# Memory attention and SwiGLU on one core: four pairs of batches swept as a wave, in an order that a table sets

## The chip, the cores and the metric

One NeuronCore of a Trainium2 chip runs one program. Its five engines have queues of their own and meet at semaphores: TensorE (PE in the profile, PEld for its weight loads), VectorE (DVE), ScalarE (ACT), GpSimd (POOL), and SyncE (SP), which issues every DMA of this kernel. The metric is the device time of one execution in microseconds (us), lower is better.

## The reference

Eight batches of eight heads attend through 32 memory slots a head; the result goes, token by token, through a gated feed-forward layer. q and k are scaled up by 200, so that the scores are sharp.

```python
a = softmax(phi, axis=2)                       # over the 576 positions
k_m, v_m = a^T k, a^T v                        # 32 x 64 a head
attn = softmax(q k_m^T / 8)                    # 576 x 32
x = (attn v_m), heads side by side             # 4608 tokens x 512
xn = x / sqrt(mean(x^2) + 1e-6) * rms_g
out = (silu(xn w_gate) * (xn w_val)) w_out     # d_ff = 1536
```

All inputs are float32 but the three weight matrices, which arrive as float64 (the kernel reads them as pairs of 32-bit words).

## The kernel before, in words

Two batches make a pair, so there are four pairs. For each pair three things are done.

**Preparation.** For each batch b: `prep` (L485) takes the maximum of phi over the positions (`mc`, then `mt` and `mr` by transposes through PE), subtracts it, and `e_bd` holds the exponentials; `kv_steps` (L556) multiplies them with k and v into `kvp`, adds the sums (`es`), normalizes (`si`, `im`, `kb`, `vb`) and turns the result (`kvt`); `km` serves the scores, `vg` and `vm` (split into a high and a low part) the sweep, `gram` the norm.

**Attention.** q is turned (`qtp`, `qT`), scored against `km` (`S`), and its softmax (`mxs` or `mx`, `ex`, `sm`) is `a`. `x_steps` (L168) turns `a` (`tp`, `at`), gets the square sum of each token by `xp` and `ssq`, takes the inverse root in `fin` (L262) by a bit trick and four Newton steps (L278) on all nine columns at once, spreads it over `at` (`rp`), and splits the result into `ath` and `atl`.

**Sweep.** An item is one pair and one of twelve columns of 128 hidden units; there are 48. `vw_steps` (L824) multiplies the values into the weights (`vp`, evacuated as `xh` on ACT and `xl` on DVE), `gv_steps` (L872) makes gate and value (`pg`, `pv`), `sg` = silu on ACT, `hf` = the product on DVE, and its split `hh` (ACT) and `hl` (POOL). After each second item `out_steps` (L918) multiplies by the two rows of w_out: nine tiles `po` of six matmuls, added into `acc` on DVE (copied on ACT the first time). All of the sweep's products are made three times over, high by high, high by low and low by high, to keep float32 accuracy.

Each weight column is made from float64 once (`convert`, L340): two passes on ACT, three on DVE (`ex`, L350, L359, L366), one addition of integers (`w`, L379, on DVE but for two on POOL), a high part on ACT and a low part on POOL (`wh`, `wl`, `oh`, `ol`, L396 and L397). It is written to DRAM (`wd`, `od`) and read again by `reload` (L410) when its buffers have been given to others: there are two sets of each.

The work stands in two stages. In the first (L422 to L803) all eight batches are prepared and pairs 0 and 1 attend, with `kv`, `q` and PSUM pools of its own. What pairs 2 and 3 need later goes through DRAM (`vgd`, `gd`). Then the pools close, and the sweep begins. It runs over pairs 0 and 1 together (two items of pair 0, two of pair 1, with the same two columns, then the next columns), and after twelve columns over pairs 2 and 3 (`where`, L817). Pairs 2 and 3 attend between the items of the first half (`attend_steps`, L959; `x2`, L1035). The place of each step is a number in `PRM` (L26): the steps are sorted by it (L802, L1088), and the framework's scheduler makes each engine's queue out of that.

Of the kernel before, what the change touches and what calls it, by code (L numbers as in the profile page):

```python
# [19 lines left out]
XTTR = True  # L20

# [3 lines left out]
WB = 3  # L25
PRM = dict(  # L26
    K_AT=[12.08, 15.05, 41.68, 67.52, 100.72, 122.69, 147.6, 167.28],
    KP=0.82,
    POST=[-0.15, 3.05, 3.9, 7.72, 15.27, 21.96],
    P1=4.13,  # L30
    PREP=[-1.56, 0.79, 2.32, 3.9, 18.7],
    PD=[2.1, 11.67, 7.79, 18.42, 7.54, 2.17],
    EXP=[1.89, 13.89, 3.07, 6.96, 11.93, 1.72],
    ES=1.16,
    PH=[9.86, 15.89, 41.23, 73.43, 103.91, 132.92],
    S_AT=[32.67, 47.44, 51.02, 69.42, 103.56, 112.2, 119.41, 123.39],
    KD=[-29.43, -117.84, -35.71, -6.98, -5.97, -14.4, 0.19, -2.47, -27.9, -16.32, -19.75, -7.2, -11.66, -11.87, -26.49, -25.1, -22.49, -18.77, -23.35, -24.43, -11.42, -13.48, -5.56, -9.46, -16.01, -22.32, -10.3, -18.0, -66.41, -9.39, -2.35, -17.36],
    QD=[5.05, 6, 3, 5, 23.44, 20.6, 19, 15.8],
    PD0=0.96,
    QL=3.73,  # L40
    OL=3.83,
    QO=[-0.32, 1.73, -1.7, 0.7, 1.27, 3.23],
    SO=[3.76, 13.53, 20.6, 28.62],
    X_AT=[102.5, 152.9],
    XP=1.78,
    LAG=0.79,
    CV=114.79,
    CP=3.53,
    CV2=155.67,
    CP2=0.05,  # L50
    QE=[0, 0],
    CE=[2, 1],
    XE=[28, 29, 14, 13],
    ESN=[3, 3, 2, 3, 3, 3, 2, 3],
    SUM=[1, 0, 1, 0, 2, 1, 2, 1],
    CA=1,
    B=[2, 2, 2],
    RO=3.35,
    RS=4.63,
    RP=2.84,  # L60
    GV=[0.12, 0.256, 0.267, 0.683, 0.84, 0.979],
    VW=[-0.204, 0.03, 0.165],
    VW0=0.296,
    O=[0.115, 0.297, 0.451, 0.524, 0.954, 0.957, 1.344, 1.487, 1.518],
    PRE=[-0.525, 1.142, 1.893, 2.147, 2.545, 2.788],
    PI=0.0157,
    PSW=[1.728, 2.047, 2.009, 2.653, 2.96, 3.24],
    SU=[1.874, 3.014, 5.716, 6.6, 9.746, 12.208, 13.357, 15.533],
    AO=[0.162, 0.169, 0.192, 0.276, 0.385, 0.474, 0.562, 0.581, 0.59, 0.601, 0.728, 0.804, 1.158, 1.217],
    XB=[17.199, 22.916],  # L70
    XS=[0.1086, 0.0359],
    XM=[21.887, 24.858],
    XN=[0.012, 0.176, 0.184, 0.33, 0.33, 0.566, 0.596, 0.699, 0.766],
    LV=[22.571, 24.198],
    CB=1,
)


def weave(*lists):

    order = []
    for li, entry in enumerate(lists):
        steps, lo, hi = entry if isinstance(entry, tuple) else (entry, 0.0, 1.0)
        n = len(steps)
        for i, s in enumerate(steps):
            order.append((lo + (hi - lo) * (i + 0.5) / n, li, i, s))
    order.sort(key=lambda e: e[:3])  # L90
    for e in order:
        e[3]()
# [3 lines left out]
def kernel(  # L96
# [12 lines left out]

    nc = tc.nc
    P = 128
# [17 lines left out]
    vm = {}  # L141
    gram = {}
    gb = persist.tile([P, 2, 2, P], F32, name="gb")
    dram = ctx.enter_context(tc.tile_pool(name="dram", bufs=1, space=bass.MemoryType.DRAM))
    gram_dram = {i: dram.tile([P, 2, 2, 64], F32, name=f"gd{i}") for i in range(G, NP)}
    a_dram = {i: dram.tile([P, NT, 256], F32, name=f"ad{i}") for i in range(G, NP)}
    rinv = [persist.tile([P, NT], F32, name=f"rinv{i}") for i in range(NP)]
    at_hi, at_lo = {}, {}

    vg_dram = {b: dram.tile([P, HP, 64], F32, name=f"vgd{b}") for b in range(2 * G, B)}  # L150
    km_late = {b: persist.tile([P, HP, 64], F32, name=f"km{b}") for b in range(2 * G, B)}
    ssqs = {}
# [6 lines left out]
    def split_v(b, vg):
        pr, j = divmod(b, 2)  # L160
        for e in range(2):
            o = e ^ j
            src = vg.rearrange("p (c e) m -> p c e m", e=2)[:, :, o, :]
            hi, lo = vm[pr][:, 0, :, e, o, :], vm[pr][:, 1, :, e, o, :]
            nc.scalar.copy(hi, src)
            nc.gpsimd.tensor_tensor(out=lo, in0=src, in1=hi.bitcast(F32), op=ALU.subtract)

    def x_steps(pr, a, psum_t, psum_x, fetch=None):  # L168

        tps, xps, srcs, st = {}, {}, {}, {}  # L170
        i = pr % G

        def first():
            st["at"] = persist.tile([P, NT, 2, P], F32, tag="at", name=f"at{pr}")
            ssqs[pr] = persist.tile([P, NT], F32, tag=f"ssq{i}", name=f"ssq{pr}")
            for par in range(2):
                rows = slice(64 * par, 64 * par + 64)
                (nc.scalar.copy if pr < G else nc.sync.dma_start)(gb[rows, :, :, rows], gram[pr][rows])
# [941 lines left out]
```

## Time and profile before

| | us |
|---|---|
| median of 3 runs (lowest, highest) | 899.51 (896.29, 899.54) |
| the profiled execution, device time | 896.89 |
| its span, first to last instruction | 895.1 |
| mean granted PE clock | 0.978 |

Times in the profile are counted from the span's start. A timeline row gives the start and the length in us, engine, line and operation, "out<-in", the shape and how many; what ended an idle time stands in brackets. A row by groups ends in "busy us, mean ns of one | idle before". A row by windows gives each engine's busy us and its instructions, then the granted PE clock, the share of the DMA engines and GB/s. The profile counts a float32 matmul twice (it is done in two passes); the order counts it once.

### The profile page before, as it was taken

Reading aid. Unit: us, or ns where it says so; the run is one execution under the profiler, and the core shown is the slowest. Engines: PE = TensorE matmul, PEld = TensorE weight load, DVE = VectorE, ACT = ScalarE, POOL = GpSimd, SP = SyncE. Lnnn points to the kernel's source line nnn. Section 1 sums busy time; section 2 is a strip of 40 time slices with the busy share of each in tenths; the row PEclk is TensorE's granted clock in tenths of the full one; section 3 lists DMA queues with packets and bytes.
Section 4 is the critical chain, followed back from the end, with each engine's and each line's share of the span. In section 5 each row is a group of like instructions: output and inputs, shape, how many; then the busy total and the mean of one; then the engine's idle time right before and its main releaser. Section 6 shows DMA issues by size and latency. Waiting matters only on the chain.

```text
span 895.1 us, 15791 instructions
## 1 busy us (share of the span) xinstructions
PE 835.6 (93%) x6207; PEld 741.3 (83%) x6207; DVE 559.0 (62%) x956; ACT 422.0 (47%) x719; POOL 286.7 (32%) x242
## 2 busy tenths in 40 slices
PE   4989586999998999999999999899999999999997
PEld 4777476899987988897788997898889999999996
DVE  5577958985778868878845746622545555455543
ACT  2666435787765645656532532344333323333330
POOL 3463735533524414323422421511211112211120
PEclk9899788999999999999999999999999999999999
DMA  8987553652644422534222143502204012040046
GB/s 292 320 263 239 204 169 101 223 168 60 217 114 153 150 61 95 163 105 142 102 73 93 60 117 102 135 1 72 70 4 139 1 63 79 1 142 1 9 110 141
DMA packets 81506, 106.41 MB, mean 119 GB/s; under 512 B 34324, under 2 KB 52248, under 8 KB 81432
## 3 DMA queue, kind: packets, MB, share of 16 engines
q1 hardware_dynamic: 81432, 105.41, 38.0%
q8 instruction: 49, 0.80, 0.4%
q14 instruction: 25, 0.20, 0.1%
HBM read 73.93 MB, written 31.46 MB: 118 GB/s over the span
## 4 chain that ended last, share of the span: by engine, by line
PE 74%; DVE 10%; issue 5%; DMA 5%; ACT 4%; POOL 1%; SPq 1%; DVEq 0%; POOLq 0%; ACTq 0%
PE po L932 29%; PE pv L890 15%; PE pg L890 14%; PE vp L843 6%; PE kvp L567 3%; DMA phi<-in_phi_dram 2%; PE xp L240 2%; DVE w L379 2%; DVE xl L868 1%; DVE ex L350 1%; DMA raw<-in_moe_w_out_dram 1%; PE qtp L679 1%; PE S L700 1%; DVE acc L939 1%; DVE mc L493 1%
## 5 line engine op out<-in xcount | busy, mean ns | idle before, releaser
L913 POOL TENSOR_TENSOR hl<-hf,hh 128x512 fp32r<-128x512 f32 (+1 forms) x96 | 141.4, 1474 | 405.9 <-ACT hh L912 392.3
L939 DVE TENSOR_TENSOR acc<-po,acc 128x512 f32<-128x512 f32 x180 | 123.1, 687 | 128.2 <-PE po L932 127.6
L932 PE MATMUL po<-oh,hh 128*128 128x512 f32 x432 | 172.4, 400 | 3.0 <-DVE acc L939 2.0
L932 PE MATMUL po<-oh,hl 128*128 128x512 f32 x432 | 170.6, 395 | 0.0
L932 PE MATMUL po<-ol,hh 128*128 128x512 f32 x432 | 170.4, 394 | 0.0
L898 ACT ACTIVATE sg<-pg 128x256 f32<-128x256 f32 x192 | 78.1, 411 | 163.2 <-PE pg L890 151.6
L868 DVE TENSOR_TENSOR xl<-vp,xh 64x1024 fp32r<-64x1024 f32 x94 | 114.7, 1220 | 52.3 <-ACT xh L867 51.2
L899 DVE TENSOR_TENSOR hf<-pv,sg 128x256 f32<-128x256 f32 x192 | 85.2, 452 | 71.6 <-PE pv L890 49.0
L867 ACT CAST xh<-vp 64x1024 fp32r<-64x1024 f32 x94 | 94.8, 1008 | 49.7 <-PE vp L843 23.9
L912 ACT CAST hh<-hf 128x512 fp32r<-128x512 f32 (+1 forms) x96 | 64.7, 674 | 81.9 <-DVE hf L899 59.5
L932 PEld LDWEIGHTS po<-oh,hl 128*128 128x128 f32 x432 | 81.2, 188 | 19.3
L932 PEld LDWEIGHTS po<-oh,hh 128*128 128x128 f32 x432 | 81.1, 188 | 17.0 <-DVE acc L939 2.9
L890 PE MATMUL pg<-ath,xh 128*128 128x320 f32 (+1 forms) x384 | 87.3, 300 | 5.7 <-ACT sg L898 3.0
L932 PEld LDWEIGHTS po<-ol,hh 128*128 128x128 f32 x432 | 81.3, 188 | 11.0
L843 PE MATMUL vp<-wh,vm 128*128 128x256 f32 x384 | 85.4, 286 | 3.6 <-DVE xl L868 2.8
L890 PE MATMUL pv<-ath,xh 128*128 128x320 f32 (+1 forms) x384 | 85.0, 299 | 1.1 <-DVE hf L899 0.9
L890 PE MATMUL pg<-atl,xh 128*128 128x320 f32 (+1 forms) x384 | 84.9, 297 | 0.0
L890 PE MATMUL pg<-ath,xl 128*128 128x320 f32 (+1 forms) x384 | 84.7, 295 | 0.0
L890 PE MATMUL pv<-atl,xh 128*128 128x320 f32 (+1 forms) x384 | 84.5, 296 | 0.0
L890 PE MATMUL pv<-ath,xl 128*128 128x320 f32 (+1 forms) x384 | 83.2, 296 | 0.0
L890 PEld LDWEIGHTS pg<-ath,xh 128*128 128x128 f32 x384 | 63.5, 189 | 12.0 <-ACT sg L898 4.8
L843 PEld LDWEIGHTS vp<-wh,vm 128*128 128x128 f32 x384 | 65.4, 189 | 6.7 <-DVE xl L868 2.3
(129 smaller groups left out, 1338.3 us busy)
## 6 DMA issues: line engine op xcount, KB each, us to landing
kv<-in_k_dram SPq DMA_DIRECT2D x32, 288.0 KB, 5.2
kv<-in_v_dram SPq DMA_DIRECT2D x32, 288.0 KB, 5.8
out_dram<-acc SPq DMA_DIRECT2D x72, 128.0 KB, 2.4
raw<-in_moe_w_gate_dram SPq DMA_DIRECT2D x12, 512.0 KB, 5.0
raw<-in_moe_w_val_dram SPq DMA_DIRECT2D x12, 512.0 KB, 3.9
wd<-wh SPq DMA_DIRECT2D x12, 512.0 KB, 3.4
wd<-wl SPq DMA_DIRECT2D x12, 512.0 KB, 4.2
raw<-in_moe_w_out_dram SPq DMA_DIRECT2D x12, 512.0 KB, 4.2
```

The lines of the kernel that those rows point to most:

```text
L240: nc.tensor.matmul(xp[64 * j:64 * j + 64, P * cc:P * cc + P], st["at"][:, t, cc, 64 * j:64 * j + 64], gb[:, j, cc], start=True, stop=True,)
L567: nc.tensor.matmul(kvp[64 * par:64 * par + 64, cc, 0:128], e_bd[j][:, hp, c, :], st["kv", b, hp][:, :, 64 * c:64 * c + 64], start=(c == 0) ...
L843: nc.tensor.matmul(vp[:, e, :], lhs(l), r[:, 2 * cc + e, :], start=(n == 0), stop=(n == 2),)
L867: nc.scalar.copy(xh[rows], src)
L868: nc.vector.tensor_tensor(out=xl[rows], in0=src, in1=xh[rows].bitcast(F32), op=ALU.subtract)
L890: nc.tensor.matmul(pt[:, :N], l[:, cc, b, half * P:half * P + P], r[:, b, cc, t0:t0 + n, :].rearrange("p t x -> p (t x)"), start=(m == 0), ...
L898: nc.scalar.activation(sg[:, :N], pg[:, :N], AF.Silu)
L899: nc.vector.tensor_tensor(out=hf[:, :, b, :], in0=pv[:, :N].rearrange("p (t x) -> p t x", x=64), in1=sg[:, :N].rearrange("p (t x) -> p t x ...
L912: nc.scalar.copy(hh, hv)
L913: nc.gpsimd.tensor_tensor(out=hl, in0=hv, in1=hh.bitcast(F32), op=ALU.subtract)
L932: nc.tensor.matmul(po, l[:, tt, :], r, start=(m == 0), stop=(m == 5))
L939: nc.vector.tensor_tensor(out=accs[key], in0=po, in1=accs[key], op=ALU.add)
```

## The change

One pool arrangement serves from the first instruction on. Only pair 0's two batches are prepared and only pair 0 attends ahead of the sweep, in early pools; pairs 1, 2 and 3 are prepared, with the narrow buffers of the sweep, while earlier pairs are swept. Sweep entries (a pair and two columns) follow `ORDER`: four of pair 0, then one of pair 1, one of pair 0, and so on; the first one or two entries of a pair lie between the last ones of its forerunner. The columns are converted as pair 0 needs them, and each later use reads them from DRAM. Every step is now one part of a list (mostly one instruction each), and `ISSUE`, 3,127 numbers, gives the order in which they are issued; the scheduler is off. Smaller edits: the integer addition of `convert` is on POOL always; the inverse root is taken in two pieces (four tiles, five tiles) with three Newton steps each; the second pair's q comes by the four strided loads of the late pairs; softmax sums are always one reduction on DVE; the sums of `phi`'s exponentials always use three POOL additions; `gram` and `vg` stay on the chip.

```diff
-G = 2
+ORDER = [
+    (0, 0), (0, 1), (0, 2), (0, 3), (1, 0), (0, 4), (1, 1), (0, 5), (1, 2), (1, 3), (1, 4), (2, 0), (1, 5), (2, 1), (2, 2), (2, 3), (2, 4), (3, 0), (2, 5), (3, 1), (3, 2), (3, 3), (3, 4), (3, 5),
+]
+ISSUE = [
+    13, 33, 14, 15, 16, 34, 17, 18, 38, 1, 2, 3, 19, 4, 5, 20, 6, 8, 7, 9, 39, 40, 10, 48, 41, 22, 11, 49,
...
+def perform(tc, parts):
+    assert sorted(ISSUE) == list(range(len(parts)))
+    with tc.manual_schedule():
+        for n in ISSUE:
+            parts[n]()
...
     def where(i):
-        ps_, r = divmod(i, NU * G * 2)
-        u, r = divmod(r, G * 2)
-        pi, f = divmod(r, 2)
-        return ps_, u, ps_ * G + pi, 2 * u + f
+        p, u = ORDER[i // 2]
+        return p, u, 2 * u + i % 2
...
-            on_pool = n < 2 and kind < 2 and PRM["CE"][n] & (1 << kind)
-            (nc.gpsimd if on_pool else V).tensor_tensor(out=d["w"].bitcast(I32), in0=d["m"], in1=d["ex"], op=ALU.add)
+            nc.gpsimd.tensor_tensor(out=d["w"].bitcast(I32), in0=d["m"], in1=d["ex"], op=ALU.add)
...
-            for _ in range(4):
+            return [f0, f1, f2, f3, f4] + [newton(a) for a in range(3)]
...
+            if t == 3:
+                steps.append(fin(0, 4))
+        steps.append(fin(4, NT))
...
+    for n in range(NS):
+        new = first_use[where(n)[1]] == n // 2
+        for kind in range(3) if new else (0, 2):
+            if new:
+                add(lambda kind=kind, n=n: load_w(kind, n), convert(kind, n))
+            else:
+                add(lambda kind=kind, n=n: reload(kind, n))
```

The queues show it at three places. On PE, before the first gate product `pg0` (item 0), this stood before; `rp1` belongs to pair 1's inverse root, `kvt7` to the last batch, `vp0` and `vp1` to items 0 and 1:

```order
L209 MATMUL rp1_4_1762<-ident_58,rinv1_71 128x128 x4
L611 MATMUL kvt7_1747<-ident_58,kb7_1743 128x128 x2
L611 MATMUL kvt7_1747<-ident_58,vb7_1744 128x128 x2
L209 MATMUL rp1_8_1768<-ident_58,rinv1_71 128x128
L636 MATMUL kvt7_1747<-vt7_1758 64x64 x4
L843 MATMUL vp0_0_1804<-wh0_1361,vm0_456 128x256
...
L843 MATMUL vp1_1839<-wh1_1714,vm0_456 128x256
L890 MATMUL pg0_00_1847<-ath0_1391,xh0_1818 128x256
```

And this stands there now (`rp0` is pair 0's inverse root, `kvt2` and `kvp3` batches 2 and 3, which are pair 1):

```order
L784 MATMUL rp0_4_973<-ident_72,rinv0_105 128x128 x4
L784 MATMUL rp0_8_987<-ident_72,rinv0_105 128x128
L498 MATMUL kvt2_992<-ident_72,kb2_828 128x128 x2
L498 MATMUL kvt2_992<-ident_72,vb2_824 128x128 x2
L459 MATMUL kvp3_0_887<-ones_109,es3_819 64x1 x2
...
L445 MATMUL kvp3_1_1024<-kv3_3_942,e_bd1_123 64x128
...
L1071 MATMUL pg0_10_1053<-ath0_970,xh0_723 128x320 x2
```

Item 0's first gate product stood behind eight batches and two attending pairs, and stands behind four batches and one attending pair.

On POOL, around items 2 and 3 (`hl` is the low part of the product, `wl` and `ol` the low parts of a weight column, `ex` an attention tile), before:

```order
L397 TENSOR_TENSOR wl3_2312<-w0_3_2230,wh3_2311 128x4x128
L397 TENSOR_TENSOR wl3_2312<-w1_3_2274,wh3_2311 128x4x128
L913 TENSOR_TENSOR hl2_0_2164<-hf2_0_2105,hh2_0_2163 128x512
L913 TENSOR_TENSOR hl2_1_2316<-hf2_1_2240,hh2_1_2315 128x640
L913 TENSOR_TENSOR hl3_0_2389<-hf3_0_2331,hh3_0_2388 128x512
L1022 TENSOR_TENSOR ex2_0_2188<-ex2_0_2188,sm2_0_2325 128x576
```

and now:

```order
L966 TENSOR_TENSOR w2_1_1511<-mi2_1_1428,wex2_1_1439 128x512
L1102 TENSOR_TENSOR hl2_0_1524<-hf2_0_1443,hh2_0_1520 128x512
L983 TENSOR_TENSOR ol1_1528<-w2_1_1511,oh1_1527 128x512
L966 TENSOR_TENSOR w2_2_1606<-mi2_2_1551,wex2_2_1539 128x512
L726 TENSOR_TENSOR ex1_1_1499<-ex1_1_1499,sm1_1_1594 128x576
L966 TENSOR_TENSOR w0_4_1652<-mi0_4_1622,wex0_4_1620 128x512
L1102 TENSOR_TENSOR hl2_1_1665<-hf2_1_1609,hh2_1_1637 128x640
L983 TENSOR_TENSOR wl4_1681<-w0_4_1652,wh4_1680 128x4x128
L1102 TENSOR_TENSOR hl3_0_1722<-hf3_0_1678,hh3_0_1708 128x512
```

The additions `w` have come in, and more columns are converted between two items.

On SP, where the rows of w_out are read again after the last `po` of a pair of items, before (items 12 and 13, with outputs of pair 1 still leaving):

```order
L942 DMA out_0_dram<-acc1_7_2748 64x512 x2
L419 DMA oh12_6499<-od0_94 128x512
L419 DMA ol12_6500<-od0_94 128x512
L419 DMA oh13_6541<-od1_95 128x512
L942 DMA out_0_dram<-acc1_8_2757 64x512 x2
L419 DMA ol13_6542<-od1_95 128x512
L419 DMA wl16_7098<-wd4_86 128x1024
L419 DMA wh16_7097<-wd4_86 128x1024
```

and now (items 24 to 29; `ad3` and `qr3` are pair 3's attention):

```order
L1009 DMA oh24_6333<-od10_103 128x512
L1009 DMA ol24_6334<-od10_103 128x512
L1009 DMA oh25_6337<-od11_104 128x512
L1009 DMA ol25_6338<-od11_104 128x512
L1009 DMA wh29_6341<-wd5_86 128x1024
L1009 DMA wl29_6342<-wd5_86 128x1024
L1141 DMA out_0_dram<-acc1_0_3354 64x512 x2
L731 DMA ad3_80<-ex3_0_6348 1152x1x64
```

A set of four `oh` and `ol` served four items and now serves two: each of the four kinds is read 36 times in place of 12, and the whole queue holds 453 DMAs in place of 356.

More of the change, by code (lines that the diff above doesn't have):

```diff
@@ L159, in split_v @@
[L159 to L176, printed above, removed]
+    rinv = [persist.tile([P, NT], F32, name=f"rinv{i}") for i in range(NP)]
@@ new lines, with bank, load_rg @@
+    V.memset(e_bd[0], 0.0)
+    nc.gpsimd.memset(e_bd[1], 0.0)
+    nc.gpsimd.memset(gb, 0.0)
+    def bank(tag, name, shape=None):
+        return ps.tile(shape or [P, 512], F32, tag=tag, name=name)
+    for t in ("vw",):
+        ps.tile([P, 2, 2, 256], F32, tag="vw", name="vw_first", bufs=1)
+    for t in "gvo":
+        bank(t, f"{t}_first")
+    load = nc.sync.dma_start
+    st = {}
+    def load_rg():
+        rows = st["rg_rows"]
+        st["rg_ps"] = tp = bank("o", "rg_ps")
+        nc.tensor.transpose(out=tp[:, :HP], in_=rows, identity=ident[:HP, :HP])
@@ new lines, in put_rg, with turn_rg, small, load_phi @@
+    def put_rg():
+        V.tensor_copy(rg[0], st["rg_ps"][:, :HP])
+    def turn_rg(s):
+        return lambda: V.tensor_copy(rg[1][:, s:s + 1], rg[0][:, s ^ 1:(s ^ 1) + 1])
+    def small(b):
+        return sa if b < 2 else sl
+    def load_phi(b):
+        if b < 2:
+            t = sa.tile([P, HP, NT, M], F32, tag="phi", name=f"phi{b}")
+        else:
+            t = sl.tile([P, HP, NT, M], F32, tag="ex", name=f"phi{b}")
+        n = 2 if b == 0 else HP
+        for i in range(0, HP, n):
+            load(
+                t[:, i:i + n].rearrange("p hp c m -> p hp (c m)"),
+                phi[b].rearrange("(hp h) (p c) m -> (h p) hp (c m)", h=2, c=NT)[:, i:i + n],
+            )
+        st["phi", b] = t
@@ new lines, in x_steps, with x2, fetch, f @@
+        steps = [first(0), first(1)]
+        for t in range(NT):
+            if fetch and t % 4 == 0:
+                steps.append(fetch(t))
+            if t % 2 == 0:
+                steps += [turn(t), copy(t)]
+            steps += [mm(t), square(t)]
+            if t == 3:
+                steps.append(fin(0, 4))
+        steps.append(fin(4, NT))
+        for t0, n in ((0, 4), (4, 4), (8, 1)):
+            steps += spread(t0, n)
+        return steps
+    def x2(pr):
+        got = {}
+        def fetch(t):
+            def f():
+                for tag, t0, n in (("qr", 0, 4), ("qT", 4, 4), ("ex", 8, 1)):
+                    if t0 == t:
+                        a = sl.tile([P, n, 256], F32, tag=tag, name=f"ain{pr}_{t0}")
+                        nc.sync.dma_start(a, a_dram[pr][:, t0:t0 + n])
+                        for k in range(n):
+                            got[t0 + k] = a[:, k]
+            return f
+        return x_steps(pr, got.get, "o", "o", fetch)
@@ new lines, in f, with add @@
+            return [mm, add] + ([put] if u == NU - 1 else [])
+        return [f(t) for t in range(NT)]
+    parts = []
+    def add(*steps):
+        parts.extend(flat(list(steps)))
+    load_phi(0)
+    st["rg_rows"] = sa.tile([HP, P], F32, name="rg_rows", bufs=1)
+    load(st["rg_rows"], rms_g.rearrange("(hp r) -> hp r", r=P))
+    for hp in range(HP):
+        load_kv(0, hp)
+    load_phi(1)
+    for hp in range(HP):
+        load_kv(1, hp)
+    add(prep(0, 0, 2), prep(0, 2, 4)[:-1], prep(1))
@@ L1088 @@
[L1088 to L1089 removed]
+            add(out_steps(i))
+    perform(tc, parts)
 _INS = ['q', 'k', 'v', 'phi', 'moe_w_gate', 'moe_w_val', 'moe_w_out', 'moe_rms_g']
```

1291 lines of the change are left out of this document (563 added, 728 removed), and 169 rows, old and new, of the table ISSUE.

## Prediction

> **What bounds the kernel now.** I read the page first, then the windows. PE is busy 93% of the span, so only 59.5 us could be won by filling it; but the slices and the windows say where busy is not the same as fast.
>
> ```profile
> PE 835.6 (93%) x6207; PEld 741.3 (83%) x6207; DVE 559.0 (62%) x956; ACT 422.0 (47%) x719; POOL 286.7 (32%) x242
> PE   4989586999998999999999999899999999999997
> ...
> 0.00:50.00 50.00, 36.39 (x454) 30.70 (x456) 29.39 (x58) 23.21 (x38) 21.43 (x27) 0.90 0.89 301
> 50.00:100.00 50.00, 42.56 (x659) 35.39 (x655) 39.07 (x85) 31.38 (x55) 28.77 (x34) 0.97 0.70 233
> 100.00:150.00 50.00, 33.62 (x385) 28.75 (x386) 35.23 (x84) 19.53 (x40) 24.36 (x25) 0.79 0.44 144
> 150.00:200.00 50.00, 46.93 (x337) 43.31 (x337) 46.80 (x71) 40.55 (x69) 21.88 (x16) 0.97 0.66 203
> 700.00:750.00 50.00, 50.00 (x314) 45.79 (x313) 25.37 (x38) 17.32 (x29) 9.90 (x7) 1.00 0.20 64
> ```
>
> From 700 us on PE never stops and DVE is half idle; before 150 us PE has gaps and, in one window, a granted clock of 0.79; from 150 to 200 us DVE is as full as PE. So there are three stages with three limits. The PE timeline gives the border and the speed of dense work, the chain of waits the period of the sweep.
>
> ```profile
> 148.41 0.39 PE L890 MATMUL pg<-ath,xh 128*128 128x256 f32 x1 [2.18 <-ACT xh L856]
> ...
> 40.25 1.30 PE L700 MATMUL S<-km,qT 128*64 128x64 f32 x36
> 53.49 2.19 PE L567 MATMUL kvp<-kv,e_bd 128*64 128x128 f32 x36
> 75.52 1.09 PE L679 MATMUL qtp<-ident,qr 128*128 128x128 f32 x8
> 89.08 1.09 PE L240 MATMUL xp<-gb,at 128*64 128x128 f32 x16
> ```
>
> ```profile
> 743.35 1.87 PE po L932 x8
> 799.52 1.87 PE po L932 x8
> 875.84 14.02 PE po L932 x60
> ```
>
> 743.35 to 799.52 is one period of four items: 56.17 us, 14.04 an item, 674 for 48. Preparing and attending one pair costs, at the dense rates above (144 records of kvp at 0.061, 144 of S at 0.036, 63 turns at 0.136, 72 of xp at 0.068, small things 3), about 30 us, four pairs 121. So PE needs 795 us. The order puts 86 of them ahead of the first gate product, which came at 148.4: 62 us lost there. The other 709 ended at 889.9 (875.84 + 14.02): 741.5 us, 32 lost. The last 5.2 us are the final addition and the output's DMA. 62 + 32 + 5 is what stands between 795 and 895.
>
> **The change, part by part.** The PE work stays at 795: the same matmuls in sweep and attention, only 48 fewer one-column sums. What moves is the work ahead of the first gate product: two more batches than pair 0 needs, one attending pair and two first columns, 44 us of PE in place of 86. What limits that stage is DVE.
>
> ```profile
> 13.35 2.11 DVE L493 TENSOR_REDUCE mc<-phi 128x128 f32<-128x1152 f32 x1 [3.92 <-DMA phi<-in_phi_dram]
> 41.63 0.75 DVE L711 TENSOR_REDUCE mxs<-S 128x18 f32<-128x576 f32 x1
> 67.64 1.35 DVE L526 TENSOR_TENSOR phi<-phi,mr 128x1152 f32<-128x1152 f32 x1 [3.02 <-PE mr L517]
> ```
>
> Summing the instructions that the order puts on DVE before that product, each by its mean here, gives 114.6 us before and 72.6 now (half of `mc`, `phi`, `mxs`, `xp`; the same 5 conversions). Before, DVE thus stood idle for 148.4 - 114.6 = 34 us, in waits such as the two above, and I keep the part of pair 0's own chain: phi's load, the turn back, scores after both batches. Idle 13: the first gate product at **86**. Bounds: 78, if only the start's 4 us and the last split (about 1.5) wait, and 94, if DVE idles in the old proportion (72.6 x 148.4 / 114.6).
>
> The early sweep, items 0 to 8, gets denser. The columns now come due with every two items, so 21 of 36 conversions fall in it, together with pair 1's whole attention.
>
> ```profile
> L868 DVE TENSOR_TENSOR xl<-vp,xh 64x1024 fp32r<-64x1024 f32 x94 | 114.7, 1220 | 52.3 <-ACT xh L867 51.2
> L899 DVE TENSOR_TENSOR hf<-pv,sg 128x256 f32<-128x256 f32 x192 | 85.2, 452 | 71.6 <-PE pv L890 49.0
> L939 DVE TENSOR_TENSOR acc<-po,acc 128x512 f32<-128x512 f32 x180 | 123.1, 687 | 128.2 <-PE po L932 127.6
> L366 DVE SCALAR_TENSOR_TENSOR ex<-raw,ex 128x512 int32<-128x512 int32 x36 | 33.7, 937 | 0.6
> L350 DVE TENSOR_SCALAR ex<-ex 128x512 f32<-128x512 f32 x36 | 23.4, 651 | 10.9 <-ACT ex L349 10.6
> L359 DVE TENSOR_SCALAR ex<-ex 128x512 int32<-128x512 int32 x36 | 21.9, 607 | 0.6
> L379 DVE CUSTOM_DVE_ANT_0 w<-mi,ex 128x1024 uint16<-128x1024 uint16 x34 | 34.6, 1018 | 2.9 <-POOL wl L397 1.1 <-DVE ex L366 0.5 <-POOL ol L397 0.3
> L379 POOL TENSOR_TENSOR w<-mi,ex 128x512 int32<-128x512 int32 x2 | 2.5, 1270 | 1.3 <-DVE u L279 0.7 <-DVE ex L366 0.6
> ```
>
> DVE: 21 x 2.2 for conversions (the addition, 1.02 each, has left), 17 `xl` x 1.22, 34 `hf` x 0.45, 18 `acc` x 0.69, and 37 of pair 1's softmax, norm and scaling: 131 us. PE: 130. ACT: 115, with 9 table loads. POOL: 98, of which 27 are the 21 additions (1.27 each). In the old order the same nine items had PE 112, DVE 99, ACT 98 and POOL 44 between their products. Now DVE and PE are both near their limit, ACT and POOL not far from it, so PE alone can't set the pace here. DVE's own 131 is the floor; what it waits for POOL comes on top. That DVE does wait is in the spread (least, median, most ns) of two kinds of instruction with both inputs in SBUF:
>
> ```profile
> L366 DVE SCALAR_TENSOR_TENSOR ex<-raw,ex x36: 634/693/2043, 87.5 to 434.6; 128x512 int32<-128x512 int32 x36
> ...
> L279 DVE TENSOR_TENSOR u<-rinv x16: 156/170/1185, 96.7 to 562.7; 128x9 f32<-128x9 f32 x16
> ```
>
> Their excess over the median grows by about a POOL instruction. A conversion's mean over its medians is some 0.65 us (0.24 of it in this `ex`, 937 against 693) where POOL is busy for 21.88 of 50; at 98 of 140 it would be 1.04, times 21 is 8 us. I take **140** for the nine items (131 to 155).
>
> Behind item 8 the remaining PE work is 795 - 44 - 130 = 621, with DVE at 376. Before, the sweep lost 32 us, most of it where conversions and attention stood between items; now most of these are done by then and I take **15** (5 to 30). The reloads: 24 more of each kind, 1.5 MB a column, 38 MB in all on 106.
>
> ```profile
> wh<-wd SPq DMA_DIRECT2D x12, 512.0 KB, 6.1
> oh<-od SPq DMA_DIRECT2D x12, 256.0 KB, 4.1
> ...
> 627.07 4.41 DMA oh<-od
> ```
>
> `wh` is asked for 12 to 30 us of PE work ahead of its use: free. `oh` and `ol` can only be asked for behind the last `po` of the items that used the buffers, and SP holds whatever is queued behind them, the next `wh` and outputs. The order leaves mostly 6 to 8 us of PE work until the next `po` (4.9 at the least); four issues and a landing take about 5.5. The old order left 4.2 in its late items and showed a trace of it only, the 4.41 above. Nothing is charged, up to 10 in the upper bound of the 15.
>
> Three Newton steps save one pass at the chain's end, but two pieces make 18 small instructions a pair for 12: no net gain, in the 72.6 and 131. Table loads go from 18 to 32; ACT has the room behind item 8.
>
> Sum: 86 + 140 + 621 + 15 + 5 = 867, and 1.8 around the span (896.9 - 895.1): **869**. The runs of before spread from 896.3 to 899.5, the profiled one near the low end, so 869 may read 2 us low against a median. The bounds together: 842 to 905.
>
> **The rivals.** (a) DVE and POOL block each other far more. The Trainium skill, SBUF — State Buffer, section Who interferes with whom, says that GpSimd and a VectorE instruction with two SBUF inputs share a port pair as an exclusive lock, and that the loser fully blocks; by that rule, moving `w` to POOL takes 1 us from DVE and lends it a longer lock. The trace agrees: 2043 against 634 ns. As a mechanism here: if each of the 63 conversion instructions waits half a POOL instruction (0.7), that is 44 in place of the 22 that my 140 holds: 22 more, and slower small steps in the first stage: **893**, hardly a gain. Against it: each is short, and POOL waits as well. (b) The order overlaps better than stage sums allow: the first gate product at 80, DVE's floor of 131, 5 lost later: 80 + 131 + 621 + 5 + 7 = **844**. For it: 50.00 of 50 in the late windows. (c) Slower: the reload of w_out. Each of the 18 late reloads stops PE when it lands later than the 7 us of cover. To eat the 30 us, each has to lack 1.7, so from a landing at 8.7 us behind the last `po` the change is even, and at 9.7 it costs 18 x 2.7 = 48: **917**. For it: one queue, and 1.5 MB more a column; against it: 64 GB/s in the late windows against 301 at the start.
>
> **How the numbers follow.** My forecast 0.60, (a) 0.16, (b) 0.16, (c) 0.06, the rest 0.02. The range for 8 in 10 takes in (b) and all but the end of (a): 844 to 891. A measurement of this kernel can tell 0.5%, 4.5 us, from no change. Faster: 0.60 + 0.16 + two thirds of (a) = 0.87. Same: 0.05. Slower: 0.08.
>
> **What would show it.** The first `pg` at 78 to 94. PE's share from there for 140 us about 0.9, DVE's over 0.9. The mean of `ex` (L366 before) over 1.1 us would be (a). A PE wait on `oh` or `ol` of over 1 us, 18 times, would be (c). The last 200 us at 14.04 an item. Wrong would be a first `pg` past 100, or PE idle for more than 30 us behind item 8.

## The result, and the profile after

| | before | after |
|---|---|---|
| median of 4 runs (lowest, highest) | 898.28 (896.29, 899.54) | 885.32 (883.80, 885.73) |
| ratio, 95% interval | | 0.9855 (0.9829 to 0.9880) |
| the profiled execution, device time | 896.89 | 883.80 |
| its span | 895.1 | 882.0 |

The kernel is 1.45% faster, 13 us. Forecast were 869, some 28 us less than the profiled execution of before: the sign is right, the size is less than half of it. The span is 15.0 us longer than the 867 of the sum.

The page of after, TensorE's share and its slices:

```profile
PE 834.2 (95%) x6175; PEld 735.5 (83%) x6175; DVE 523.7 (59%) x1015; ACT 434.0 (49%) x730; POOL 322.7 (37%) x266
PE   4878898999999999999999999999999999999997
PEclk9988999999999999999999999999999999999999
```

The forecast's stages are windows here: up to the first gate product, items 0 to 8, the rest. First after, then before (columns: window; busy us of PE, PEld, DVE, ACT, POOL; granted clock, DMA share, GB/s).

```profile
0.00:82.60 82.60, 56.93 (x722) 49.00 (x722) 61.11 (x160) 44.56 (x77) 44.07 (x45) 0.92 0.72 243
82.60:231.70 149.10, 139.08 (x1052) 121.29 (x1051) 112.93 (x227) 105.75 (x183) 94.89 (x77) 0.99 0.67 206
231.70:876.60 644.90, 638.20 (x4405) 565.18 (x4403) 348.91 (x629) 283.72 (x472) 183.76 (x145) 1.00 0.48 145
```

```profile
0.00:148.40 148.40, 111.44 (x1486) 93.91 (x1486) 102.14 (x225) 72.98 (x131) 72.95 (x83) 0.89 0.68 227
148.40:269.60 121.20, 116.79 (x832) 106.80 (x833) 94.80 (x143) 89.90 (x153) 49.27 (x35) 0.99 0.54 160
269.60:889.90 620.30, 607.33 (x3891) 540.63 (x3889) 361.38 (x589) 259.09 (x436) 164.50 (x125) 1.00 0.28 85
```

The first stage came as forecast, at 82.6 (86, bounds 78 to 94). The nine items took 149.1 in place of 140, the rest up to TensorE's end 644.9 in place of 636, the tail 5.4 in place of 5. -3.4 + 9.1 + 8.9 + 0.4 = 15.0: the whole miss lies in the sweep, in equal parts up to item 8 and from item 9 on.

"PE 638.20 of 644.90" doesn't show it, because records overlap and a slow stretch counts as busy. So I took the distance from each TensorE record's start to the next one's, less the median distance of its kind (0.232 us for a po, 0.147 for a gate product of 320 columns, 0.119 for 256). What is left over is lost. (Ahead of the first gate product, where short products of many kinds stand, the count depends on how the kinds are formed; by the forecast's own 86 and 44 us of TensorE's work the losses there are 62 and 39.) In us, with the gaps over 0.15 us and the smaller ones apart for the sweep:

```text
          first pg   lost ahead   lost items 0-8   lost items 9-47   of the sweep: gaps >0.15   smaller
before     148.4        58             10.1             25.7               24.2                  11.2
after       82.6        37             20.4             24.2               22.9                  21.3
```

The change wins some 21 us ahead of the sweep and gives 9 back in it. The forecast let the sweep lose 25 us, 10 in items 0 to 8 and 15 behind; it loses 44.6, against 35.8 before. Behind item 8 it loses as much as before, in another way: the gaps over 0.15 us fall from some 18 to 10 us, and the smaller ones grow from some 7 to 14. The largest waits of TensorE in items 0 to 8 have these causes (columns: who waited, for whom, us in all, times, longest):

```profile
PE pg L1071 <- DVE xl L1051: 3.4, 2, 3.1
PE po L1128 <- DVE ex L705: 2.0, 2, 1.1
PE xp L819 <- DVE ssq L831: 1.3, 1, 1.3
PE qtp L672 <- DMA qr<-in_q_dram: 1.2, 2, 0.9
PE qtp L672 <- ACT qT L678: 1.0, 2, 0.8
```

These are many short waits, on VectorE, ScalarE and a DMA, and none of the engines is full: VectorE was busy for 113 of 149 us, and 131 had been called its floor. Neither of the two rivals with a single cause shows in them. No TensorE wait on a reload is in the trace. VectorE's `wex` (`ex` at L366 before) got shorter, not longer: its mean is 786 ns against 937, in this spread (least, median, most):

```profile
L959 DVE SCALAR_TENSOR_TENSOR wex<-raw,wex x36: 636/692/1668, 27.1 to 355.3; 128x512 int32<-128x512 int32 x36
...
L959 DVE SCALAR_TENSOR_TENSOR wex<-raw,wex 128x512 int32<-128x512 int32 x36 | 28.3, 786 | 0.9
```

The smaller gaps are twice those of before, and the trace puts no waits beside them. They were the first thing to explain.

### The profile page after: what moved, and what is told of

The parts are those of the page before. It is cut to its first block, busy times and chain, and to the rows that moved or that the text cites. A ratio compares the mean times of both kernels' runs of the same rounds, so it can differ in the third digit from the quotient of the medians.

```text
span 882.0 us, 15810 instructions
## 1 busy us (share of the span) xinstructions
PE 834.2 (95%) x6175; PEld 735.5 (83%) x6175; DVE 523.7 (59%) x1015; ACT 434.0 (49%) x730; POOL 322.7 (37%) x266
## 4 chain that ended last, share of the span: by engine, by line
PE 77%; DVE 7%; ACT 7%; DMA 5%; issue 2%; SPq 1%; POOL 0%; DVEq 0%; ACTq 0%; POOLq 0%
PE po L1128 30%; PE pg L1071 15%; PE pv L1071 15%; PE vp L1034 7%; PE kvp L445 4%; ACT xh L1053 3%; DVE xl L1051 3%; DMA phi<-in_phi_dram 2%; PE xp L819 2%; PE qtp L672 1%; PE S L690 1%; DMA qr<-in_q_dram 1%; DVE acc L1137 1%; DMA kv<-in_v_dram 1%; PE kvp L459 1%
## 5 line engine op out<-in xcount | busy, mean ns | idle before, releaser
L1102 POOL TENSOR_TENSOR hl<-hf,hh 128x512 fp32r<-128x512 f32 (+1 forms) x96 | 138.0, 1439 | 340.6 <-ACT hh L1097 319.5
L1087 DVE TENSOR_TENSOR hf<-pv,sg 128x256 f32<-128x256 f32 (+1 forms) x192 | 84.8, 453 | 120.1 <-PE pv L1071 72.1
L1082 ACT ACTIVATE sg<-pg 128x256 f32<-128x256 f32 (+1 forms) x192 | 77.4, 410 | 157.0 <-PE pg L1071 115.3
L1071 PE MATMUL pv<-ath,xh 128*128 128x256 f32 (+1 forms) x384 | 86.9, 307 | 0.7 <-DVE hf L1087 0.5
L1071 PE MATMUL pg<-ath,xl 128*128 128x256 f32 (+1 forms) x384 | 83.1, 298 | 3.4 <-DVE xl L1051 3.4
L1071 PE MATMUL pg<-ath,xh 128*128 128x256 f32 (+1 forms) x384 | 86.3, 306 | 0.0
L1071 PE MATMUL pv<-ath,xl 128*128 128x256 f32 (+1 forms) x384 | 82.2, 295 | 0.0
L1071 PE MATMUL pg<-atl,xh 128*128 128x256 f32 (+1 forms) x384 | 82.1, 295 | 0.0
L1071 PE MATMUL pv<-atl,xh 128*128 128x256 f32 (+1 forms) x384 | 81.8, 294 | 0.0
L1071 PEld LDWEIGHTS pv<-ath,xh 128*128 128x128 f32 x384 | 62.8, 189 | 9.4 <-issue 2.1
```

The lines of the kernel that those rows point to most:

```text
L1071: nc.tensor.matmul(pt[:, :N], l[:, cc, b, half * P:half * P + P], r[:, b, cc, t0:t0 + n, :].rearrange("p t x -> p (t x)"), start=(m == 0), ...
L1082: nc.scalar.activation(sg[:, :N], acts[gi, b, 0][:, :N], AF.Silu)
L1087: V.tensor_tensor(out=acts[gi][:, :, b, :], in0=acts[gi, b, 1][:, :N].rearrange("p (t x) -> p t x", x=64), in1=acts[gi, b, 2][:, :N].rearr ...
L1102: nc.gpsimd.tensor_tensor(out=hl, in0=acts[gi].rearrange("p t b x -> p t (b x)"), in1=hsplit[i, gi][0].bitcast(F32), op=ALU.subtract,)
```

## The experiments

**What a small gap is.** In the trace TensorE loses 0.09 us each time that it goes from the sweep's products to the key, score or norm products of the preparation, and 0.10 on the way back. Two things set these apart: they are two-pass float32, and they are half as wide (128\*64), in pairs that write rows 0 to 63 and 64 to 127 side by side. My first theory was that the change between one pass and two costs the time. Three kernels insert a tiny matmul ahead of each of 126 po groups, where TensorE is full.

```diff
                 pt[0] = po = bank("o", f"po{i}_{t}")
                 m = 0
+                for _ in range(1 if i >= 20 else 0):
+                    nc.tensor.matmul(po[:, :64], hsplit[i - 1, gi][0][:, 0, :].bitcast(F32),
+                                     wosplit[i - 1][0][:, :64].bitcast(F32), start=True, stop=True)
```

Expected of one two-pass product, of two, and of one that is one-pass (no bitcast):

> The changed kernel, with one 64-column two-pass (float32) matmul put ahead of each po group of items 20 and later (126 of them, into the tile that the group then overwrites); the outputs stay. Theory: each change of TensorE between one-pass and two-pass products costs 0.09 us by the trace (po then kvp 0.33 against po then po 0.23). Every insertion makes two changes and adds about 0.05 us of work: 126 x (0.18 + 0.05) = 29 us more than the changed kernel's 885, so 914. Rival, that a change costs nothing and the small gaps come from DMA traffic: 126 x 0.05 = 6 us, 891.

> The same with two such matmuls in a row at each of the 126 places: twice the work and the same number of changes. Theory: 126 x (0.18 + 0.10) = 35 us, 920, so only 6 us more than with one. Rival, no price on a change: 126 x 0.10 = 13 us, 898.

> The same 126 insertions, one each, but one-pass like the products around them: no change of kind. Theory: 126 x 0.05 = 6 us, 891 (up to 126 x 0.12 = 15 if the weight load of 128 rows shows). Rival: the same 891. If this costs as much as the two-pass insertion, the theory of the changes falls.

Measured: 911.34, 937.56 and 897.64, that is 26, 52 and 12 us over the changed kernel's 885.32. Two cost twice what one costs, so the changes of kind have no price and the theory fell: such a short product costs 0.1 us a pass, whether it is of its neighbours' kind or not. The trace of the first shows why (start, length, operation; PEld is the load of the weights):

```profile
781.69 0.46 PE L1071 MATMUL pv<-ath,xl 128*128 128x320 f32 x2
781.98 0.33 PE L1124 MATMUL po<-oh,hh 128*128 128x64 f32 x2
782.12 0.48 PE L1133 MATMUL po<-oh,hh 128*128 128x512 f32 x1
782.44 0.40 PE L1133 MATMUL po<-ol,hh 128*128 128x512 f32 x1
...
781.84 0.33 PEld L1124 LDWEIGHTS po<-oh,hh 128*128 128x128 f32 x2
782.09 0.19 PEld L1133 LDWEIGHTS po<-oh,hh 128*128 128x128 f32 x1
```

The insertion starts on time (781.98, two products of 0.147 after 781.69): its weights began to load at 781.84. The po behind it takes 0.32 to the next in place of 0.23. Its weights began to load at 782.09, 0.03 ahead of its start, and a load takes 0.19: so short a product doesn't cover it.

Then the width, by one half-width product, and by two:

```diff
+                for _ in range(1 if i >= 20 else 0):
+                    nc.tensor.matmul(po[:64, :64], hsplit[i - 1, gi][0][:, 0, :64],
+                                     wosplit[i - 1][0][:, :64], start=True, stop=True)
```

> The changed kernel with one 64-column one-pass matmul of half width (64 of 128 output rows, as the profile's 128*64) ahead of each of the 126 po groups of items 20 and later. The earlier insertions showed no price on one-pass against two-pass; the trace shows 0.09 us each time that TensorE goes from a 128*128 to a 128*64 product or back (pv then kvp 0.21 to 0.24 against pv then pv 0.12 to 0.15; kvp then pg 0.20 against 0.10). Theory: 126 x (2 x 0.09 + 0.03) = 26 us over the changed kernel's 885.3, so 912. Rival, that only a short matmul's uncovered weight load costs: as the full-width insertion, 12 us, 898.

> The same with two half-width matmuls in a row: the same two changes of width a place. Theory: 126 x 0.03 to 0.06 = 4 to 8 us over the run with one, 916 to 920. Rival: twice the one's excess over 885.3.

Measured: 897.79 and 903.53. One costs what a full-width one costs (897.64), and the second adds 5.7 us, less than either forecast for two. Width alone has no price either. In the trace of one, its weights load ahead of it, while a full-width product runs:

```profile
781.45 0.14 PEld L1124 LDWEIGHTS po<-oh,hh 128*64 128x64 f32 x1
...
781.56 0.19 PE L1124 MATMUL po<-oh,hh 128*64 128x64 f32 x1
```

The products of the preparation are both half-width and two-pass, and stand in pairs:

```diff
+                for h in range(2 if i >= 20 else 0):
+                    nc.tensor.matmul(po[64 * h:64 * h + 64, :64], hsplit[i - 1, gi][0][:, 0, :64].bitcast(F32),
+                                     wosplit[i - 1][0][:, :64].bitcast(F32), start=True, stop=True)
```

> The changed kernel with a pair of 64-column two-pass products ahead of each of the 126 po groups of items 20 and later: output rows 0 to 63 and 64 to 127, as the key and score products of the preparation have them. Neither two passes nor half width alone had a price of its own. Theory: going from full-width products to such a side-by-side pair costs 0.09 us and going back 0.10, since the pair's weights are only loaded when the product before has ended, and the next weights when the pair has; the pair itself takes 4 records of 0.036 = 0.14 by the score products. 126 x 0.33 = 42 us, 927; from po to the pair 0.33 us in the trace where po to po takes 0.23. Rival (a short product's weight load is the whole price, as in the runs before): with the two side by side 26 us, 911, and 0.23 from po to the pair.

Measured: 935.40, 50 us, 0.40 a place; expected were 42 by the theory, 26 by the rival. The price is there. Whether it is the pair's was still open, so one half-width product alone, in two passes (the half-width insertion with the bitcast):

> The changed kernel with one half-width, two-pass 64-column product alone (rows 0 to 63) ahead of each of the 126 po groups of items 20 and later. Theory (the price is that of two products side by side): as the full-width two-pass product, 26 us over 885.3, so 911. Rival (the price is that of half width together with two passes): 0.19 us more a place, 26 + 24 = 50 us, 935, as the pair.

Measured: 934.70, as much as the pair. So the theory of the pair fell as well: what costs is a product that is half-width and two-pass at once, and a second one beside it is free. In the trace of this run:

```profile
801.98 0.40 PE L1071 MATMUL pv<-ath,xl 128*128 128x256 f32 x2
802.31 0.33 PE L1124 MATMUL po<-oh,hh 128*64 128x64 f32 x2
802.57 0.50 PE L1133 MATMUL po<-oh,hh 128*128 128x512 f32 x1
802.91 0.39 PE L1133 MATMUL po<-ol,hh 128*128 128x512 f32 x1
```

From 801.98 the two pv take 0.235; the insertion starts at 802.31, 0.09 late, where the full-width one had started on time. From it to the po behind it 0.26 pass, where the full-width one had taken 0.14. The weight loads (PEld) show where this comes from:

```profile
801.87 0.31 PEld L1071 LDWEIGHTS pv<-ath,xl 128*128 128x128 f32 x2
802.31 0.19 PEld L1124 LDWEIGHTS po<-oh,hh 128*64 128x64 f32 x2
802.57 0.19 PEld L1133 LDWEIGHTS po<-oh,hh 128*128 128x128 f32 x1
802.68 0.19 PEld L1133 LDWEIGHTS po<-ol,hh 128*128 128x128 f32 x1
```

And the same at a stretch of kvp in the changed kernel:

```profile
473.22 0.31 PEld L1071 LDWEIGHTS pv<-ath,xl 128*128 128x128 f32 x2
473.67 0.64 PEld L445 LDWEIGHTS kvp<-kv,e_bd 128*64 128x64 f32 x12
474.47 0.30 PEld L1071 LDWEIGHTS pg<-ath,xh 128*128 128x128 f32 x2 [0.17 <-issue]
```

```profile
473.33 0.40 PE L1071 MATMUL pv<-ath,xl 128*128 128x256 f32 x2
473.67 0.88 PE L445 MATMUL kvp<-kv,e_bd 128*64 128x128 f32 x12
474.47 0.50 PE L1071 MATMUL pg<-ath,xh 128*128 128x256 f32 x2
```

The weights of pv, and of the second po, load while the product ahead of them runs. Those of the half-width two-pass product start with the product itself (802.31, 473.67), and so do those of the first product behind it (802.57, 474.47): at both ends nothing is loaded ahead. The Trainium skill, TensorEngine Tiling (Array Packing), section Key Properties, says that changing the tiling mode drains TensorE. The trace agrees for these products, at 0.09 us in and 0.10 out (in the stretch above, the two pg from 474.47 take 0.50, where the two pv from 473.33 take 0.40); for the one-pass half-width product it shows nothing of the kind.

Behind the first gate product, the changed kernel enters such a stretch 67 times, the kernel before 28 times. 17 of the 67 lie in items 0 to 8 and 50 behind, against 6 and 22. 39 x 0.19 is 7.4 us of the 10 that the smaller gaps grew by.

The direct test moves 23 of these stretches to the next one, by the table alone (a kvp chunk, a score or a norm product that nothing in between needs). One place of the table, where 432 to 435 are `kvp` products of one block; 2197 (a pv), 2200 (a pg) and 2176 (a po) stood between them:

```diff
-    432, 1367, 2179, 2197, 433, 2199, 2200, 434, 2202, 2176, 461, 462, 435, 2177,
+    1367, 2179, 2197, 2199, 2200, 432, 433, 434, 435, 2202, 2176, 461, 462, 2177,
```

> The changed kernel with another table alone: 23 stretches of key, score and norm products (side by side, half width) in the sweep are moved to the next such stretch, over 0.7 to 2.8 us of sweep products, where no instruction in between needs them. 23 of 67 stretches go. Theory: each stretch less saves 0.19 us: 4.4 us faster, 881 (879 to 883). Rival (the small gaps have nothing to do with the order): no change, 885. Rival (what is moved comes too late for VectorE, whose queue then holds TensorE up): slower, 887 and more.

Measured: 881.25, ratio to before 0.9806 (0.9780 to 0.9832): 4.1 us under the changed kernel, as the theory had it. 44 stretches are left. The trace splits the gain: counted as above, the smaller gaps lose some 7 us less, 0.3 a stretch and not 0.19, and the gaps over 0.15 us some 4 us more. So the price of a stretch is shown, and that the sum met the theory is in part luck. This is the fastest kernel here that computes the whole reference: it beats the kernel before, and five of its six executions are shorter than every one of the changed kernel's.

**VectorE's queue.** The additions go back to VectorE:

```diff
-            nc.gpsimd.tensor_tensor(out=d["w"].bitcast(I32), in0=d["m"], in1=d["ex"], op=ALU.add)
+            V.tensor_tensor(out=d["w"].bitcast(I32), in0=d["m"], in1=d["ex"], op=ALU.add)
```

> The changed kernel with the integer addition of all 36 conversions back on VectorE. Theory (the two engines hold each other up little, and TensorE waits in items 0 to 8 because VectorE's queue is in a fixed order): VectorE gets 36 x 1.02 = 37 us more, 21 of the 36 in items 0 to 8, where it is busy 113 of 149 us; the work ahead of TensorE's waits gets longer: 4 to 15 us slower, 889 to 900. Rival (the shared port: the additions on GpSimd block VectorE): 36 GpSimd instructions fewer to wait for, so no change or up to 10 us faster, 875 to 885.

Measured: 899.82, ratio to before 1.0020 (1.0000 to 1.0040). The move of `w`, which the forecast gave no price, is worth 14.5 us in this order: without it nothing of the gain is left. The rival of the shared port is out as the larger effect. The additions take 823 ns on VectorE here and 1284 on GpSimd, and it still pays. Of the 15.9 us between the two spans, 1.9 arise ahead of the first gate product and 10.9 in items 0 to 8, where TensorE's gaps over 0.15 us grow from some 13 to 24 us.

Less work on VectorE, by leaving out the clamp of the exponent in each conversion:

```diff
-            V.tensor_scalar(
-                out=ex.bitcast(F32), in0=ex.bitcast(F32), scalar1=EXP_LO, scalar2=EXP_HI,
-                op0=ALU.max, op1=ALU.min,
-            )
```

> The changed kernel without the clamp of the exponent in each conversion (one VectorE instruction of 0.56 us, 36 times; the inputs here don't need it). VectorE loses 20 us, 12 of them in items 0 to 8. Theory (what TensorE waits for in items 0 to 11 stands behind conversions in VectorE's queue; the addition cost 14.5 us for 29.6 us of VectorE, 0.5 us each): 6 to 10 us faster, 875 to 879. Rival (these waits come from PSUM tiles and the latency of the chain, not from VectorE's queue): within 2 us, 883 to 887.

Measured: 881.22, 4.1 us less. It lies between the theory and the rival: 20 us of VectorE give 0.2 us each, where the additions gave 0.5. The length of VectorE's queue is part of these waits, not all; the rest of what the additions cost stays unexplained.

The longest of the waits, 3.12 us at 106 us, looked like a matter of queue order. VectorE in the changed kernel:

```profile
100.04 1.22 DVE L1051 TENSOR_TENSOR xl<-vp,xh 64x1024 fp32r<-64x1024 f32 x1 [0.83 <-ACT xh L1053]
101.19 0.47 DVE L705 TENSOR_TENSOR ex<-S,mx 128x320 f32<-128x320 f32 x1
101.58 0.41 DVE L940 TENSOR_SCALAR wex<-wex 128x512 f32<-128x512 f32 x1
102.03 1.48 DVE L952 TENSOR_SCALAR wex<-wex 128x512 int32<-128x512 int32 x1
103.54 0.69 DVE L959 SCALAR_TENSOR_TENSOR wex<-raw,wex 128x512 int32<-128x512 int32 x1
...
105.06 1.23 DVE L1051 TENSOR_TENSOR xl<-vp,xh 64x1024 fp32r<-64x1024 f32 x1
```

The second `xl` has its input at 100.0 and starts at 105.06, behind conversions, one of which took 1.48 in place of 0.43 while a GpSimd instruction ran (101.94 to 103.23). One number of the table, moved, puts it ahead of them:

```diff
-    1485, 1484, 1453, 319, 1080,
+    1485, 1484, 1486, 1453, 319, 1080,
...
-    494, 1459, 1486, 519, 1085,
+    494, 1459, 519, 1085,
```

(1484 and 1486 are the two halves of `xl2`.)

> The changed kernel with one instruction moved in the table: the second half of item 2's low part xl, which VectorE starts at 105.06 us though its input has been there since 100.0, and for which TensorE waits 3.12 us. It now stands ahead of three conversion steps and two score steps. Theory (this wait is the fixed order of VectorE's queue): TensorE's wait at 103 to 106 us goes, and 2 to 3 us of it last to the end: 882 to 883. Rival (the conversions and scores that now come 1.2 us later hold TensorE up instead): the wait comes back within the next two items, 885.

Measured: 885.22. The rival is right: TensorE's wait there is 0.3 us now, others stand in its place (1.7 us for `sg` at 107.6, 1.0 for a `qtp`), and item 9 starts at 232.2 against 231.7. A wait in this stage isn't a single late instruction; TensorE, VectorE and ScalarE wait for one another in turn. The granted clock is 0.90 in the window from 102.5 to 120.1 us of the changed kernel, and 1.00 in those beside it, so this stretch also loses by a slower TensorE; with the instruction moved it is 0.90 there still.

**Newton steps.** The forecast had no net gain of them. A fourth step, in each of the two pieces (`last` ends the third step and makes the fourth):

```diff
-                    if a == 0:
+                    if "u" not in t:
...
-                return [g0, g1, g2]
+                def last():
+                    g2()
+                    g0()
+                    g1()
+                    g2()
+                return [g0, g1, g2 if a < 2 else last]
```

> The changed kernel with a fourth Newton step in each of the eight inverse roots, as the kernel before has it: 24 more VectorE instructions of 0.15 to 0.2 us, 0.5 us in each chain. Theory (one chain of four stands ahead of the first gate product and is waited for there): 0.5 to 1.5 us slower, 886 to 887, which a measurement cannot tell from none. Rival (each chain is waited for by the norm and scaling products of its pair in the sweep, too): 4 us and more, 889.

Measured: 890.38, 5.1 us more (3.4 by the ratios to before, 0.9893 against 0.9855); the rival's side. The first gate product comes at 86.2 in place of 82.6, and pair 1's chain delays items 5 to 9 by 2.8 more. Those of pairs 2 and 3 cost nothing.

**The same edits in the old order, and the order without them.** First the additions on GpSimd in the kernel before:

```diff
-            on_pool = n < 2 and kind < 2 and PRM["CE"][n] & (1 << kind)
-            (nc.gpsimd if on_pool else V).tensor_tensor(
+            nc.gpsimd.tensor_tensor(
```

> The kernel before with one part of the change alone: the integer addition of every conversion on GpSimd. In the changed kernel this move is worth 14.5 us. Theory (the addition lengthens VectorE's queue wherever conversions stand ahead of what TensorE waits for): before has 5 or 6 of its conversions ahead of the first gate product and the rest spread over 270 us, so less: 3 to 8 us faster than before, 891 to 896. Rival (the gain needs the new order, where 21 conversions stand in 149 us): no change, 897 to 901. Rival of the shared port: slower, over 901.

Measured: 889.66, ratio 0.9893 (0.9879 to 0.9908), 9.3 us less than before and more than the theory allowed. In its trace the first gate product is at 151.6 and the sweep loses 26 us in place of 36. The scheduler laid all queues anew for it, so the 9.3 us hold what the new layout gives, too. Then both small edits in the old order (with the line below as well), and neither in the new one (on the changed kernel, the additions back on VectorE and a fourth step, as in the diffs above):

```diff
-            for _ in range(4):
+            for _ in range(3):
```

> The kernel before in its old order with both small edits: all additions on GpSimd (889.7 alone) and three Newton steps. Theory (one inverse root of four, 3 steps fewer of 0.16 us each, is waited for ahead of the first gate product and one at 563 us): 0.5 to 1.5 us less, 888 to 889, so the small edits give 10 to 11 of the 14 us in the old order too. Rival (the Newton steps are worth as much as in the changed kernel): 885.

> The changed kernel with both small edits undone: the additions on VectorE and four Newton steps. What stays of the change is the wave, its table of issue and the inverse root in two pieces. Theory (the two prices add up: 885.3 + 14.5 + 5.1): 905, that is 6 us slower than before, so the new order alone loses. Rival (the two overlap, since both lengthen VectorE's queue ahead of the same products): 897 to 901, no change.

Measured: 891.35, ratio 0.9931 (0.9904 to 0.9957), and 902.47, ratio 1.0054 (1.0033 to 1.0076). All of it in one table, as ratios to before:

| additions | Newton steps | old order | wave and its table |
|---|---|---|---|
| VectorE | 4 | 1 | 1.0054 (1.0033 to 1.0076) |
| VectorE | 3 | | 1.0020 (1.0000 to 1.0040) |
| GpSimd | 4 | 0.9893 (0.9879 to 0.9908) | 0.9893 (0.9866 to 0.9919) |
| GpSimd | 3 | 0.9931 (0.9904 to 0.9957) | 0.9855 (0.9829 to 0.9880) |

The new order by itself is half a per cent slower; with the additions on GpSimd and four steps it is worth nothing against the old one with the same edit; only with both small edits does it beat the old one's best, by 0.4%, at the edge of the intervals. The trace of the order alone has its first gate product at 85.4, so what it wins ahead of the sweep is there; items 0 to 8 then take 161.9 us, against 149.1 with both edits and 121.2 before. In the old order, where the scheduler lays everything anew, the missing fourth step gains nothing (0.4% the other way). The table was the same one in all four kernels of the right column (a fourth step rides on the third): no run has a table laid for additions on VectorE, so this table is what gives nothing without the edits, and whether a wave must is not shown.

**DMA.** Every column that is read again is read twice:

```diff
-            nc.sync.dma_start(t[a].bitcast(F32), src[:, a])
+            for _ in range(2):
+                nc.sync.dma_start(t[a].bitcast(F32), src[:, a])
```

> The changed kernel with every weight column that is read again read twice, into the same buffers: 54 MB more of DMA, 199 MB in all, and twice the issues ahead of the next po. Theory (the reloads cost TensorE nothing, since the trace has no wait on them and 6 to 8 us of TensorE's work stand ahead of the next po): 0 to 5 us slower, 885 to 890, with first waits on oh or ol. Rival (DMA traffic is what slows the sweep, 145 MB in place of 106): the added 54 MB cost more than 39 MB did, 13 us and more, 898.

Measured: 1159.55. Neither theory had it, and it isn't a test of traffic: the second reading of a buffer waits on SP for the first to land, so the four readings of w_out come one after the other (the queue's issues, then a wait of SP and two of TensorE: us in all, times, longest):

```profile
805.75 2.92 SPq L1010 DMA_DIRECT2D oh<-od  x2
808.73 3.26 SPq L1010 DMA_DIRECT2D ol<-od  x2
812.04 3.82 SPq L1010 DMA_DIRECT2D oh<-od  x2
815.91 3.71 SPq L1010 DMA_DIRECT2D ol<-od  x2
...
SPq L1010 <- DMA oh<-od: 103.2, 36, 6.5
...
PE po L1129 <- DMA oh<-od: 64.5, 21, 6.0
PE po L1129 <- DMA ol<-od: 63.7, 25, 3.5
```

That is 14 us in place of some 1.6 until the last is issued, with 6 to 8 of cover: TensorE waits 128 us for `oh` and `ol`, and its mean granted clock falls to 0.88 from 0.99. It is the slower rival's mechanism, past the point from which it decides. So once more, with copies that have no wait, into DRAM that nobody reads:

```diff
             nc.sync.dma_start(t[a].bitcast(F32), src[:, a])
+            x = dram.tile([P, 512], F32, name=f"again{kind}_{n}_{a}")
+            nc.sync.dma_start(x, (src[:, a] if kind == 2 else src[:, a].rearrange("p hp g f -> p (hp g f)"))[:, :512])
```

> The changed kernel with a copy beside every reload: behind each of the 144 reading DMAs a second one moves 256 KB of the same column to a place of its own in DRAM that nobody reads, 38 MB read and 38 MB written more, with no wait of its own. Theory (traffic as such costs TensorE nothing as long as the reads land within their 6 to 8 us of cover): within 3 us, 885 to 888. Rival (the added 39 MB of the change are what slows the sweep): 38 to 76 MB more cost 10 us or more, 895 and up.

Measured: 907.34, 22 us more. By its size this is the rival's, but the trace says otherwise: behind item 8 the gaps over 0.15 us grow from 9.6 to 28.5, the smaller ones from 14.1 to 16.0. TensorE isn't slowed; it waits, mostly for readings that now land behind a copy (first dmax, then the changed kernel, from 232 us on):

```profile
PE po L1130 <- DMA ol<-od: 8.2, 9, 1.4
PE po L1130 <- DMA oh<-od: 3.2, 4, 1.1
PE po L1130 <- DVE acc L1139: 1.6, 3, 0.8
```

```profile
PE po L1128 <- DVE acc L1137: 1.6, 3, 0.8
PE po L1128 <- ACT acc L1135: 1.4, 2, 0.8
PE po L1128 <- ACT qT L678: 1.0, 1, 1.0
```

So the cover of the reloads holds in the changed kernel, with little to spare.

## Why the prediction was right in direction and wrong in size

The step that failed is the loss in the sweep: the sum put it at 10 us in items 0 to 8 and 15 behind, and it was 20.4 and 24.2. Two things are in it that the sum had at nothing or too small: the price of each stretch of half-width two-pass products, and the short mutual waits of items 1 to 5.

- **The first gate product at 86** (78 to 94): right, 82.6. Counting VectorE's work in the order, plus the pair's own chain, was good to 4 us: VectorE's records ahead of it add up to 69 us, forecast were 72.6. (They overlap, so the window above has 61.) But the 82.6 hold a gain that I had set at nothing: with a fourth Newton step it was 86.2.
- **Items 0 to 8 in 140** (131 to 155): 149.1, inside the bounds, wrong in its reason. "DVE's own 131 is the floor" failed: VectorE's records add up to 122 us, and to 113 with their overlaps counted once, so its share was 0.76, where over 0.9 was to show. The 9 us that the sum of the records falls short are the conversions, 37 us in place of 21 x 2.2 = 46. TensorE's dense 129 was the larger sum, and 20 us of short waits and gaps came on top, not 10.
- **15 behind item 8** (5 to 30): 24, inside the bounds, and failed in its reason. "Most of these are done by then" is so for conversions, and the large gaps did shrink to some 10 us. It isn't so for the preparation and attention of pairs 2 and 3, which the wave spreads over the sweep up to 620 us. There their half-width two-pass products break TensorE's stream, 50 times in place of 22: at 0.19 us at the least, some 9.5 of the 24 us, for which the sum had no term. Taking 23 of the 67 away brought 4.1 us.
- **The moved addition** stood in the sum as 1 us less for VectorE a conversion, with GpSimd's longer lock as a rival. It could have been priced in the old order: there the same edit alone, with the queues laid anew, gives 9.3 us. And the order, to which the forecast gave the whole gain, gives none without it in this table.
- **"Three Newton steps ... no net gain"**: 5.1 us in the new order (3.4 by the ratios), by the chain ahead of the first gate product and pair 1's.
- **Rival (a)**, 893 by the shared port: out. The Trainium skill, SBUF — State Buffer, section Who interferes with whom, lets VectorE and GpSimd block each other; single instructions do show it (1.48 for 0.43), but undoing the move costs 14.5 us. The mean of `wex` is 786 ns with the additions on GpSimd and 843 with them on VectorE in the new order, and 939 and 937 in the old: most of its fall is the order's, and more GpSimd work lengthened it in neither.
- **Rival (b)**, 844: its 80 came nearly true, its 5 lost in the sweep didn't.
- **Rival (c)**, slower by the reload: no wait in this kernel; dmax and dma2 show the mechanism once readings land later.
- **A slip in the bounds**: "842 to 905" takes the 1.8 around the span into the lower bound alone; the upper one is 907. Nothing hangs on it.

What stays open: which of the mutual waits of items 1 to 5 (18 of the 20 us lost) comes first, and why a microsecond of additions taken off VectorE is worth 0.5 us and one of the clamp 0.2. Moving one instruction only moved the waits.

## What to carry to other kernels

Price each small edit of a large change by itself, in the old kernel: here one line on another engine, in the old order and with its queues laid anew, gave about three quarters of the gain, and the reordering that gave the change its name, in the table that it came with, was worth nothing without it. Where TensorE is "busy" to 99%, measure the distance between starts, since neither the pipelined records nor the waits show what a mixed order costs. If small half-width products of float32 have to stand in a dense stream, put them together: each visit cost 0.2 to 0.3 us here, however short, though what is moved can then come too late for another engine.

## What the runs showed of the hardware that was not expected

- A half-width product (128\*64) in two passes doesn't have its weights loaded while the full-width product ahead of it runs, nor does the full-width product behind it while it runs itself: in the changed kernel 0.09 us are lost on the way in, and 0.10 by the first product behind. One such product costs what two side by side cost (934.70 and 935.40). A half-width product in one pass has no such price (897.79 against 897.64 at full width), nor has a full-width one in two passes (911.34). Why only both together have it is open.
- A full-width 64-column product in a stream of longer ones costs 0.10 us a pass (12.3 us for 126), some three times its distance of 0.03 to the next start: the weights of the product behind it begin to load only 0.03 ahead of its start, and that one takes 0.32 to the next in place of 0.23.
- In this program, a second DMA into the same buffer held SP until the first had landed (SP waited 103 us for `oh` alone): the four readings of w_out, each made twice, took 2.9 to 3.8 us each, 14 us until the last was issued in place of 1.6.
